# Linear attention and a squared-ReLU MLP on one core: batch 2's first matmul in the plain form, the last output matmul in another order, and new numbers in the planner

## The chip, the cores and the metric

The kernel runs on one core of a Trainium2 chip. Five engines work side by side, each on its own instructions in order: TensorE (PE in the profile; PEld is its loading of weights), VectorE (DVE), ScalarE (ACT), GpSimd (POOL) and SyncE (SP). DMA transfers are issued from the queues of SP, POOL and ACT. The metric is the device time of the core in microseconds (us), the median of several runs.

## The reference

There are 8 batches of 8 heads, 576 positions and 64 features per head. First comes a linear attention (no softmax), then a two-layer MLP over all 4608 rows of 512:

```python
def phi(x, c, s):                       # c, s: cos and sin of pi/2 * position / 576
    r = np.maximum(x, 0.0)
    return np.concatenate([r * c, r * s], axis=-1)
q_p, k_p = phi(q, cos_w, sin_w), phi(k, cos_w, sin_w)
kv  = einsum('bhsf,bhsd->bhfd', k_p, v);  z = k_p.sum(axis=2)
num = einsum('bhsf,bhfd->bhsd', q_p, kv)
den = einsum('bhsf,bhf->bhs', q_p, z)[..., None] + 1e-06
x   = (num / den)                       # heads side by side: 4608 x 512
h   = x @ w_in                          # 512 -> 2048
g   = np.maximum(h, 0.0) ** 2
out = g @ w_out                         # 2048 -> 512
```

## The kernel before

**Tiling.** Each batch has 512 main rows (four tiles j of 128) and 64 tail rows. The tails of all eight batches make a ninth block of 512 rows, m = 8, which goes through the MLP last. So the MLP has nine blocks of 512 rows; weights and activations are bf16, sums are float32 in PSUM (six banks numbered 0 to 5, and a pair called abank for the attention).

**The attention of a batch** (`plan_att`, L1005): SP loads v, k and q in halves (`load_half`, L176); ACT or DVE, whichever is free, make the cosine and sine features (`feat`, L278 and L282) and cast v (L300); TensorE forms kv and z in abank (`att_kv`, L324), ACT copies them out (L335); the features of q are transposed by a DMA on SP's queue (`att_qT`, L348), or by TensorE for some early tiles; `att_num` (L375) multiplies, `att_div` (L393 to L399) divides on DVE, and the result x is transposed again, by a DMA (`att_x`, L416) or by TensorE and a copy (L421, L425). Batch 1's x goes by TensorE.

**The MLP of a block** has a first matmul (`gemm1`) and an output matmul (`gemm2`). In the plain form, the first matmul is 16 units of 128 columns of w_in, each with 4 matmuls over all 512 rows (`unit_mm`, L460), an ACT relu (L469) and a DVE square of four units at a time (L477). In the other form the product of 2 x 2 blocks is made of seven block products instead of eight, numbered 1, 2, 5, 6, 7, 3, 4 in `plan_gemm1_7` (L864). It needs sums of blocks of w_in made once (`w1_sum`, L495; one of them overwrites a block of w_in), and of x for each batch (`x_sum`, L519). Per group of two column blocks there are seven products of 4 matmuls of 256 columns (`in_product`, L537), an ACT copy of product 5 (L907), two "seeds" in which ACT copies a partial sum from one bank to another (L896), two relus (L553), two DVE additions (L560), a maximum (L569) and one square (L477). There are four groups a batch. The output matmul has the same seven products (`product`, L686), each as two halves of 8 matmuls, with sums of the blocks of g (`g_sum`, L665) and of w_out (`w2_sum`, L646), a copy of product 5 (L977), two seeds (L951) and four result blocks (L957 on DVE, L961 on ACT). Blocks 0 and 1 have their first matmul in the plain form; `FIRST_7 = 2` (L1103) says that batch 2 is the first in the other. Block 0's output matmul is plain too (`first_out`, L602).

**The order of the work** after the first 17 us is made when the kernel is built. `Plan.add` notes each operation with its engine, a planned duration, what it reads and writes, and for TensorE's a due time. `Plan.order` (L55) goes through planned time: on the engine that is free first, of the operations that are ready, it takes the one with the earliest due time; due times are also passed back from what needs a result. An operation's result is ready a planned lag after its end (`LAG`, L23, or one of its own for a DMA). The order that comes out is the order of instructions on every engine. On the chip, the engines wait for each other's real results. Planned stages ("windows") follow each other: in window b there are the output matmul of block b, the first matmul of block b + 1 and the attention of batch b + 2.

**The end.** The last block's output matmul uses banks 0, 1 and 4. Its four result blocks are stored apart, each in two DMAs for 64 partitions (`put_part`, L631): two blocks on POOL's queue, one on SP's, and the last block one DMA on SP's and one on ACT's.

Of the kernel before, what the change touches and what calls it, by code (L numbers as in the profile page):

```python
# [9 lines left out]
ALU = mybir.AluOpType  # L10
# [8 lines left out]
class Plan:  # L19

    LAG = {"PE": 0.24, "ACT": 0.1, "DVE": 0.1, "POOL": 0.1, "SP": 0.1}  # L23

# [85 lines left out]
def kernel(  # L110
# [9 lines left out]
    nc = tc.nc  # L120
# [438 lines left out]
    def in_add(m, i, j, u, to):  # L559
# [65 lines left out]
    def put_part(i, eng, g, c0, c1):  # L625
        dst = bass.AP(
            tensor=out.tensor,
            offset=((4 * i + g) * S + MAIN) * DM + c0,
            ap=[[DM, TAIL], [2 * S * DM, 2], [1, c1 - c0]],
        )  # L630
        eng.dma_start(out=dst, in_=y_of(B, i)[g * TAIL : (g + 1) * TAIL, :, c0:c1])  # L631

    def w2_block(j, c):
# [92 lines left out]
    def plan_load(b, nm, after=0.0):  # L726
        for half in range(2):
            add("SP", 1.66, lambda half=half: load_half(nm, b, nc.sync, half),
                w=[(nm, half)], lag=2.0 + (CARE if b == 2 else CARE_IN), after=after)

    def plan_load_tail(b, nm, after=0.0):
        add("SP", 0.6, lambda: load_tail(nm, b, nc.sync), w=[(nm + "t", b % 2)], lag=2.0 + (CARE if b in (2, 3) and nm != "q" else CARE_IN), after=after)

# [59 lines left out]
    def plan_qT_pe(b, j, to, due, eng):  # L793
        slot = n_P[0] % 3
        n_P[0] += 1
        add("PE", 8 * 0.057, lambda: att_qT_pe(b, j, 0, H, to), r=q_parts((j,)), w=[("bank", to)], due=due)
        add(eng, cost(eng, 1024, "psum") if eng == "ACT" else 0.69, lambda: att_qT_copy(b, j, 0, H, to, ENG[eng]),
            r=[("bank", to)], w=[("qpTp", slot)])
        where[b, j] = ("qpTp", slot)
# [9 lines left out]
    def plan_x(b, i):  # L809
        js = (2 * i, 2 * i + 1) if i < J // 2 else (J,)  # L810
        w = [("xT", b % 2, j) for j in js] if i < J // 2 else [("xT8", b // 2)]
        if i < J // 2:
            add("SP", 1.5, lambda: att_x(b, i), r=[x_key(j) for j in js], w=w, lag=2.5 + CARE)
        else:
            add("SP", 1.2, lambda: att_x(b, i), r=[x_key(j) for j in js], w=w, lag=2.0 + CARE)

    def plan_x_pe(b, j, to, due, eng):
        add("PE", 4 * 0.057, lambda: att_x_pe(b, j, to), r=[x_key(j)], w=[("bank", to)], due=due)
        add(eng, cost(eng, 512, "psum") if eng == "ACT" else 0.42, lambda: att_x_copy(b, j, to, ENG[eng]),
            r=[("bank", to)], w=[("xT", b % 2, j)])  # L820
# [18 lines left out]
    def plan_gemm1(m, t, dt, banks, plain=False):  # L839
        order = list(range(HB)) if plain else [hb for h in range(HB2) for hb in (h, h + HB2)]  # L840
        for n, hb in enumerate(order):
            plan_unit(m, hb, banks[n % len(banks)], t + n * dt, halves=plain and n < 3)
            u = n // 4
            k = 2 if plain and u == 3 else 4
            if n % k == k - 1:
                a = n % 4 + 1 - k
                add("DVE", 0.15 + 512 * k * 0.00053, lambda u=u, a=a, k=k: square(m, u, plain, a, k),
                    w=[key for x in order[n + 1 - k : n + 1] for i in range(2) for key in g_keys(m, i, x // HB2, (x % HB2,))])
            if n % 4 == 3:
                if u >= 2 if plain else u % 2:  # L850
                    c = u - 2 if plain else u // 2
                    plan_g_sums(m, 4 * c, 4 * c + 4)

    def plan_w1_sums(after):
        first, second = [("w1", 0), ("w1", 1)], [("w1", 2), ("w1", 3)]
        for n, r, w in (
# [4 lines left out]
        ):  # L861
            add("DVE", 1.24, lambda n=n: w1_sum(n), r=r, w=w, after=after)

    def plan_gemm1_7(m, t, dt):  # L864
# [6 lines left out]
        for n, r, w in (  # L871
# [4 lines left out]
        ):  # L876
            add("DVE", 0.42, lambda n=n: x_sum(m, n), r=r, w=w)
        lo, hi = [("w1", 0), ("w1", 1)], [("w1", 2), ("w1", 3)]
# [5 lines left out]
        for u in range(HB2 // 2):  # L884
# [17 lines left out]
            def plus(a, i, j):  # L902
                add("DVE", 0.69, lambda u=u: in_add(m, i, j, u, a), r=[("bank", a)] + five, w=g(i, j))

# [5 lines left out]
            prod(6, Y)  # L910
            relu(X, 0, 0)
            seed(Y, X)
            prod(7, X)
            prod(3, Y)
            plus(X, 1, 1)
            plus(Y, 1, 0)
            prod(4, X)
            relu(X, 0, 1)
            add("DVE", 0.42, lambda u=u: in_max(m, u), w=g(1, 0) + g(1, 1))
            add("DVE", 1.24, lambda u=u: square(m, u, False), w=[key for i in range(2) for j in range(2) for key in g(i, j)])  # L920
            if u % 2:
                plan_g_sums(m, 2 * u - 2, 2 * u + 2)

    def plan_g_sums(m, h0, h1):
        hs = range(h0, h1)
        g = lambda i, j: g_keys(m, i, j, hs)
        s = lambda n: [("gs", n, h) for h in hs]
        dur = 0.15 + 256 * (h1 - h0) * 0.00053
        for n, r, w in (
# [7 lines left out]
    def plan_gemm2(m, t, dt):  # L937
# [35 lines left out]
        X, Y = (4, 5) if m < B else (0, 1)  # L973
        Z = X if m < B else 4
        prod(1, X)
        prod(5, Y)
        add("ACT", cost("ACT", 512, "psum"), lambda: nc.scalar.copy(out=five_of(m)[:, :, :], in_=half_bank(Y)),  # L977
            r=[("bank", Y)], w=[("five",)])
        seed(X, Y)
        prod(6, Y)  # L980
        prod(2, X)
        last(X, 0, 0, False)
        seed(Y, Z)
        if m == B:
            store_half(0, 0, ("POOL", "POOL"))
        prod(7, Z)
        prod(3, Y)
        last(Z, 1, 1, True)
        last(Y, 0, 1, True)
        if m < B:  # L990
            store(0)
        else:
            store_half(1, 1, ("POOL", "POOL"))
            store_half(0, 1, ("SP", "SP"))
        prod(4, Z)
        last(Z, 1, 0, False)
        if m == B:
            store_half(1, 0, ("SP", "ACT"))
        else:
            store(1)  # L1000

# [30 lines left out]

    for i, at in enumerate((16.0, 19.5, 22.0, 24.5)):
        plan.given["w1", i] = at
# [4 lines left out]
    tB = tA + HB * dtB  # L1039
    for nm, at in (("q", 30.0), ("k", 35.2), ("v", 40.0)):  # L1040
        plan.given.update({(nm, half): at for half in range(2)})
    plan.given.update({("kt", 1): 36.0, ("vt", 1): 40.5})
    for i, at in enumerate((33.0, 38.0, 42.5, 45.0)):
        plan.given["w2", i] = at

    def plan_first(s):
        half, hq = s // 4, s % 4
        js = (2 * half, 2 * half + 1)
        for a in range(2):
            to = 2 * (s % 2) + a  # L1050
            add("PE", 8 * 0.1092, lambda a=a: first_mm(s, P if s in (0, 4) else W, a),
                r=[("xT", 0, j) for j in js] + [("w1", hq)], w=[("bank", to)], due=T0 + (s + a / 2) * dt0)
            add("ACT", 0.59, lambda a=a: first_relu(s, a), r=[("bank", to)],
                w=[("g", 0, half, hb // HB2, hb % HB2) for hb in range(4 * hq + 2 * a, 4 * hq + 2 * a + 2)])
        add("DVE", 0.69, lambda: first_square(s),
            w=[("g", 0, half, hb // HB2, hb % HB2) for hb in range(4 * hq, 4 * hq + 4)])
# [33 lines left out]
    for n in range(1, 5):  # L1090
        for c in range(2):
            p = {1: 5, 2: 6, 3: 7, 4: 4}[n]
            before = {1: [], 2: [("w2t", 5, c)], 3: [], 4: [("w2t", 6, c)]}[n]
            add("DVE", 0.69, lambda n=n, c=c: w2_sum(n, 4 * c, 4 * c + 4),
                r=before + ([("w2", 2 + c)] if n == 3 else [("w2", c), ("w2", 2 + c)]),
# [15 lines left out]
    for b in range(2, B):  # L1111
# [108 lines left out]
```

## Time and profile before

| what | value |
|---|---|
| time, median of 3 runs | 284.98 us (284.95 to 285.75) |
| the profiled execution | 282.78 us, of which the span of instructions 281.0 us |
| TensorE busy | 267.0 us, 95% of the span |
| VectorE busy | 225.6 us, 80% |
| ScalarE busy | 196.8 us, 70% |
| granted clock of TensorE | 1.0 |
| moved by DMA | 53.38 MB, mean 190 GB/s |

The profile is one execution. Busy times are sums over instructions; matmuls overlap in the array, so the end shown for a matmul lies after the start of the next. In the lines of the timeline the columns are: start in us from the span's start, length, engine, line of the kernel, operation, what it writes and reads, the shapes, how many instructions the line merges, and in brackets the idle time of the engine before it with what ended it.

### The profile page before, as it was taken

The page shows a single profiled execution, that of the slowest core. Times are in us where ns is not written, and L with a number is a line of the kernel's source. Part 1 is how long each engine was busy: PE and PEld are TensorE (multiplying, and loading weights), DVE is VectorE, ACT ScalarE, POOL GpSimd, SP SyncE. Part 2 cuts the span into 40 slices and gives each one's busy share as a digit, 9 for nine tenths or more (in the row PEclk, how much of TensorE's full clock was granted, in tenths as well). Part 3 has the DMA queues.
Part 4 walks back from the last instruction along what each step waited for, and adds up shares of the span by engine and source line. Part 5 has one row for each costly group of instructions (what it writes and reads, how often), then busy time and mean ns, then how long its engine had stood idle before and what let it go on. Part 6 is the DMA issues. An engine that isn't in the chain of part 4 may idle for free.

```text
span 281.0 us, 6788 instructions
## 1 busy us (share of the span) xinstructions
PE 267.0 (95%) x2755; PEld 220.2 (78%) x2755; DVE 225.6 (80%) x437; ACT 196.8 (70%) x352; POOL 17.8 (6%) x31
## 2 busy tenths in 40 slices
PE   8899999799999979999999999999999999999793
PEld 3578955464779869888898899898988888888682
DVE  0966855989999998899989989997899779876701
ACT  2875862887997779999989999996526455555220
POOL 8345000000000000000000000000000000000011
PEclk9999999999999999999999999999999999999999
DMA  6999999999999999999899999474123001100305
GB/s 215 324 201 284 323 246 377 219 248 281 228 307 261 266 235 271 225 348 193 251 217 245 241 250 237 99 226 77 37 40 155 17 0 77 76 2 0 152 20 130
DMA packets 83534, 53.38 MB, mean 190 GB/s; under 512 B 55856, under 2 KB 79920, under 8 KB 83504
## 3 DMA queue, kind: packets, MB, share of 16 engines
q1 hardware_dynamic: 77376, 42.35, 60.8%
q0 software_dynamic: 5984, 10.49, 15.5%
q8 instruction: 21, 0.34, 0.5%
q10 hardware_dynamic: 144, 0.13, 0.1%
q14 instruction: 9, 0.07, 0.1%
HBM read 36.70 MB, written 9.44 MB: 164 GB/s over the span
## 4 chain that ended last, share of the span: by engine, by line
PE 72%; DMA 12%; ACT 7%; POOL 3%; issue 2%; SPq 1%; DVE 1%; POOLq 0%; ACTq 0%; DVEq 0%
PE bank L686 33%; PE bank L537 29%; DMA v<-in_v_dram 6%; PE bank L460 4%; DMA k<-in_k_dram 3%; PE abank L375 3%; DMA q<-in_q_dram 3%; PE abank L324 2%; SPq L176 1%; ACT kp L278 1%; ACT vext L300 1%; ACT qp L278 1%; ACT qpTp L907 1%; ACT bank L896 1%; PE bank L444 1%
## 5 line engine op out<-in xcount | busy, mean ns | idle before, releaser
L553 ACT ACTIVATE gT<-bank 128x512 bf16<-128x512 f32 x56 | 32.9, 599 | 33.4 <-PE bank L537 33.1
L686 PEld LDWEIGHTS <-gT 128*128 128x128 bf16 x512 | 49.3, 98 | 6.9 <-DVE gT L477 0.8
L537 PE MATMUL bank<-xT,w1sb 128*128 128x256 bf16 x336 | 48.9, 272 | 2.4 <-ACT bank L896 2.3
L686 PE MATMUL bank<-w2sb,gT 128*128 128x256 bf16 x384 | 49.8, 273 | 0.5 <-DVE gT L477 0.5
L537 PEld LDWEIGHTS <-w1sb 128*128 128x128 bf16 x448 | 42.7, 98 | 8.7 <-issue 3.4
L560 DVE TENSOR_TENSOR gT<-bank,qpTp 128x512 bf16<-128x512 f32 x56 | 37.6, 685 | 9.9 <-PE bank L537 8.5
L686 PEld LDWEIGHTS <-gs 128*128 128x128 bf16 x384 | 37.0, 98 | 6.5 <-issue 1.4
L477 DVE TENSOR_TENSOR gT<-gT 128x2048 bf16<-128x2048 bf16 (+1 forms) x33 | 38.9, 1187 | 3.9 <-ACT gT L553 3.5
L537 PEld LDWEIGHTS <-w1t 128*128 128x128 bf16 x336 | 32.4, 98 | 3.6
L686 PE MATMUL bank<-w2t,gs 128*128 128x256 bf16 x256 | 33.5, 273 | 1.3 <-ACT bank L951 1.3
L896 ACT COPY bank<-bank 128x512 f32<-128x512 f32 x56 | 32.4, 587 | 0.9 <-PE bank L537 0.5
L537 PE MATMUL bank<-qpTp,w1t 128*128 128x256 bf16 x224 | 32.8, 272 | 0.0
L399 DVE TENSOR_TENSOR x<-abank,rden 128x512 bf16<-128x512 f32 x31 | 21.4, 691 | 1.1
L957 DVE TENSOR_TENSOR ysb<-bank,y 128x512 f32<-128x512 f32 x16 | 11.0, 684 | 10.1 <-PE bank L686 9.9
L907 ACT COPY qpTp<-bank 128x512 f32<-128x512 f32 x28 | 16.3, 593 | 2.6 <-PE bank L537 2.4
L631 POOL DMA_DIRECT2D out_dram<-ysb x4 | 2.4, 614 | 245.3 <-ACT ysb L961 243.8
L278 ACT ACTIVATE kp<-k,sin_col 128x512 bf16<-128x512 f32 x23 | 16.3, 724 | 2.2 <-DMA k<-in_k_dram 2.2
L537 PE MATMUL bank<-xT,w1t 128*128 128x256 bf16 x112 | 16.8, 273 | 0.0
L537 PE MATMUL bank<-zeros,w1sb 128*128 128x256 bf16 x112 | 16.8, 272 | 0.0
L278 ACT ACTIVATE qp<-q,cos_col 128x512 bf16<-128x512 f32 x19 | 13.6, 722 | 4.4 <-DMA q<-in_q_dram 4.4
L686 PE MATMUL bank<-w2sb,gs 128*128 128x256 bf16 x128 | 16.6, 273 | 0.0
L686 PE MATMUL bank<-w2t,gT 128*128 128x256 bf16 x128 | 16.5, 273 | 0.0
(98 smaller groups left out, 414.9 us busy)
## 6 DMA issues: line engine op xcount, KB each, us to landing
out_dram<-ysb SPq DMA_DIRECT2D x16, 512.0 KB, 3.1
v<-in_v_dram SPq DMA_DIRECT2D x12, 512.0 KB, 6.3
q<-in_q_dram SPq DMA_DIRECT2D x12, 512.0 KB, 5.6
k<-in_k_dram SPq DMA_DIRECT2D x12, 512.0 KB, 6.1
v<-in_v_dram POOLq DMA_DIRECT2D x2, 1024.0 KB, 12.4
w1sb<-in_moe_w_in_dram POOLq DMA_DIRECT2D x4, 512.0 KB, 12.9
w2sb<-in_moe_w_out_dram POOLq DMA_DIRECT2D x4, 512.0 KB, 15.4
k<-in_k_dram SPq DMA_DIRECT2D x1, 1024.0 KB, 6.1
```

The lines of the kernel that those rows point to most:

```text
L278: eng.activation(out=dst[ps, :, lo : lo + D], in_=src[ps], func=ACTF.Relu, scale=col[ps])
L375: nc.tensor.matmul(out=num[half][ps, hh * E1 : (hh + 1) * E1], lhsT=qpT[half][:, hh, ps], rhs=kvzs[b2][:, half * HH + hh, :], start=True, ...
L399: nc.vector.tensor_tensor(out=x[:, a:z], in0=n4[:, :, :, 0:D].rearrange("p b (k l) d -> p b k l d", l=2), in1=rden[:, a:z] .rearrange("p b ...
L460: nc.tensor.matmul(out=out_, lhsT=w1sb[:, kb, hb * P : (hb + 1) * P], rhs=x_block(m, kb), start=(kb == 0), stop=(kb == KB - 1),)
L477: nc.vector.tensor_tensor(out=g, in0=g, in1=g, op=ALU.mult)
L537: nc.tensor.matmul(out=bank[to][:, s * W : (s + 1) * W], lhsT=lhs[:, kb, (2 * u + s) * P : (2 * u + s + 1) * P], rhs=rhs[:, kb, :], start= ...
L553: nc.scalar.activation(out=g_pair(m, i, j, u), in_=bank[to][:, :].rearrange("p (s c) -> p s c", s=2), func=ACTF.Relu,)
L560: nc.vector.tensor_tensor(out=g_pair(m, i, j, u), in0=bank[to][:, :].rearrange("p (s c) -> p s c", s=2), in1=in_five(u).rearrange("p (s c) ...
L686: nc.tensor.matmul(out=bank[to][:, s * DM2 : (s + 1) * DM2], lhsT=lhs[:, hb, s * P : (s + 1) * P], rhs=rhs[:, hb, :], start=(fresh and hb ...
L896: add("ACT", psum, lambda: nc.scalar.copy(out=bank[b][:, :], in_=bank[a][:, :]), r=[("bank", a)], w=[("bank", b)])
L907: add("ACT", psum, lambda u=u, Y=Y: nc.scalar.copy(out=in_five(u), in_=bank[Y][:, :]), r=[("bank", Y)], w=five)
L957: lambda: nc.vector.tensor_tensor(out=y_view(m, i, cc), in0=half_bank(a), in1=five_of(m)[:, :, :], op=ALU.add),
```

## The change

Three things change. `FIRST_7` goes from 2 to 3, so batch 2's first matmul takes the plain form and the sums of w_in are made for batch 3. In block 8, the last group of the first matmul squares its blocks apart, and the output matmul adds its products in the order 1, 2, 6, 5, 7, 3, 4 with banks 0, 1, 5 and 4; its last result block is copied in two halves and stored in four DMAs, three on SP's queue and one on ACT's. The planner's durations, lags, arrival times of loads, and some due times get other numbers; the due times of batch 1's attention become earlier. A branch for `FIRST_7 == 1` is added that isn't taken.

```diff
-    LAG = {"PE": 0.24, "ACT": 0.1, "DVE": 0.1, "POOL": 0.1, "SP": 0.1}
+    LAG = {"PE": 0.31, "ACT": 0.15, "DVE": 0.14, "POOL": 0.1, "SP": 0.1}
...
+    def square_block(m, i, j, u):
+        g = g_pair(m, i, j, u)
+        nc.vector.tensor_tensor(out=g, in0=g, in1=g, op=ALU.mult)
+
+    def square_half(m, u):
+        g = gT_of(m).rearrange("p (j h) c -> p j h c", j=2)[:, :, 2 * u : 2 * u + 2, W : 2 * W]
+        nc.vector.tensor_tensor(out=g, in0=g, in1=g, op=ALU.mult)
...
+    def put_quarter(i, eng, g, s_, c0, c1):
+        dst = bass.AP(
+            tensor=out.tensor,
+            offset=((4 * i + 2 * s_ + g) * S + MAIN) * DM + c0,
+            ap=[[DM, TAIL], [1, c1 - c0]],
+        )
+        eng.dma_start(out=dst, in_=y_of(B, i)[g * TAIL : (g + 1) * TAIL, s_, c0:c1])
+
+    def last_copy(s_, to):
+        nc.scalar.copy(out=y_view(B, 1, 0)[:, s_, :], in_=half_bank(to)[:, s_, :])
...
         if kind == "feat":
-            return {"ACT": 0.2 + 0.00083 * n, "DVE": 0.16 + 0.0005 * n}[eng]
+            return {"ACT": 0.185 + 0.00083 * n, "DVE": 0.14 + 0.0005 * n}[eng]
         if kind == "cast":
-            return {"ACT": 0.19 + 0.00083 * n, "DVE": 0.09 + 0.00077 * n}[eng]
+            return {"ACT": 0.095 + 0.00083 * n, "DVE": 0.08 + 0.0005 * n}[eng]
         if kind == "psum":
-            return {"ACT": 0.155 + 0.00085 * n, "DVE": 0.15 + 0.00105 * n}[eng]
-        return 0.15 + 0.00053 * n
+            return {"ACT": 0.045 + 0.00085 * n, "DVE": 0.06 + 0.00105 * n}[eng]
+        return 0.06 + 0.00053 * n
...
-        add("SP", 2.95 if i < J // 2 else 1.48, lambda: att_qT(b, i), r=q_parts(js),
-            w=[("qpT", i)], lag=CARE + (1.3 if i < J // 2 else 2.5))
+        add("SP", 2.0 if i < J // 2 else 1.5, lambda: att_qT(b, i), r=q_parts(js),
+            w=[("qpT", i)], lag=CARE + (2.4 if i < J // 2 else 1.7))
...
             prod(4, X)
+            if apart:
+                add("DVE", 0.34, lambda u=u: in_max(m, u), w=g(1, 0) + g(1, 1))
+                add("DVE", 0.60, lambda u=u: square_half(m, u), w=g(1, 0) + g(1, 1))
             relu(X, 0, 1)
+            block(0, 1)
...
+        X, Y, Z, V = 0, 1, 5, 4
         prod(1, X)
         seed(X, Y)
         prod(2, X)
         last(X, 0, 0, False)
+        store_half(0, 0, ("POOL", "POOL"))
+        prod(6, Y)
         seed(Y, Z)
+        prod(5, V)
+        five(V)
         prod(7, Z)
+        last(Z, 1, 1, True)
+        store_half(1, 1, ("POOL", "POOL"))
         prod(3, Y)
         last(Y, 0, 1, True)
+        store_half(0, 1, ("SP", "SP"))
         prod(4, Z)
+        for sub in range(2):
+            add("ACT", cost("ACT", 256, "psum"), lambda sub=sub: last_copy(sub, Z),
+                r=[("bank", Z)], w=[("y", 1, 0, sub)])
+            for g, q in enumerate(("SP", "ACT") if sub else ("SP", "SP")):
+                add(q, 0.6, lambda g=g, q=q, sub=sub: put_quarter(1, ENG[q], g, sub, 0, DM2),
+                    r=[("y", 1, 0, sub)], w=[("out", m, 1, 0, g, sub)])
...
-        plan_num(1, j, tA + (10.5 + 1.5 * j) * dtB)
+        plan_num(1, j, tA + (6.0 + 1.0 * j) * dtB)
         if j == 0:
-            plan_qT_pe(1, 3, 2, tA + 12 * dtB, "DVE")
-        plan_x_pe(1, j, 3, tA + (11.5 + 1.5 * j) * dtB, "ACT" if j % 2 else "DVE")
+            plan_qT_pe(1, 3, 2, tA + 7 * dtB, "DVE")
+        plan_x_pe(1, j, 3, tA + (7.2 + 1.0 * j) * dtB, "ACT" if j % 2 else "DVE")
...
-    win[0] = (t, t + HB * dC)
-    plan_gemm1(1, t, dC, (2, 0, 1, 3), True)
-    t += HB * dC
-    FIRST_7, STRIDE, SHIFT = 2, 2.0, -6.0
+    win[0] = (t, t + 14.0)
+    FIRST_7, STRIDE, SHIFT = 3, 2.0, -6.0
...
+        plan_gemm1(1, t, dC, (2, 0, 1, 3), True)
+        t += HB * dC
...
         if m == FIRST_7:
-            plan_w1_sums(win[m - 2][0])
+            plan_w1_sums(28.0 if m == 2 else win[m - 2][0])
```

More of the change, by code (lines that the diff above doesn't have):

```diff
@@ L861, in plan_w1_sums @@
         ):
-            add("DVE", 1.24, lambda n=n: w1_sum(n), r=r, w=w, after=after)
+            add("DVE", 1.14, lambda n=n: w1_sum(n), r=r, w=w, after=after)
     def plan_gemm1_7(m, t, dt):
@@ L902, in plus, with block @@
             def plus(a, i, j):
-                add("DVE", 0.69, lambda u=u: in_add(m, i, j, u, a), r=[("bank", a)] + five, w=g(i, j))
+                add("DVE", 0.60, lambda u=u: in_add(m, i, j, u, a), r=[("bank", a)] + five, w=g(i, j))
+            apart = m == B and u == HB2 // 2 - 1
+            def block(i, j):
+                if apart:
+                    add("DVE", 0.34, lambda u=u: square_block(m, i, j, u), w=g(i, j))
             prod(1, X)
@@ L911, in plan_gemm1_7 @@
             relu(X, 0, 0)
+            block(0, 0)
             seed(Y, X)
@@ L917, in plan_gemm1_7 @@
             prod(4, X)
+            if apart:
+                add("DVE", 0.34, lambda u=u: in_max(m, u), w=g(1, 0) + g(1, 1))
+                add("DVE", 0.60, lambda u=u: square_half(m, u), w=g(1, 0) + g(1, 1))
             relu(X, 0, 1)
-            add("DVE", 0.42, lambda u=u: in_max(m, u), w=g(1, 0) + g(1, 1))
-            add("DVE", 1.24, lambda u=u: square(m, u, False), w=[key for i in range(2) for j in range(2) for key in g(i, j)])
+            block(0, 1)
+            if not apart:
+                add("DVE", 0.34, lambda u=u: in_max(m, u), w=g(1, 0) + g(1, 1))
+            if not apart:
+                add("DVE", 1.14, lambda u=u: square(m, u, False), w=[key for i in range(2) for j in range(2) for key in g(i, j)])
             if u % 2:
```

80 lines of the change are left out of this document (44 added, 36 removed).

## The prediction

> **What bounds the kernel now.** I read the page's busy shares first, then a table of busy time by stretches, then the waits of TensorE alone, and last the timeline around each of those waits.
>
> ```profile
> span 281.0 us, 6788 instructions
> PE 267.0 (95%) x2755; PEld 220.2 (78%) x2755; DVE 225.6 (80%) x437; ACT 196.8 (70%) x352; POOL 17.8 (6%) x31
> ```
>
> TensorE is busy for 95% of the span, so this is a TensorE-bound kernel; what can be won is the few places where it stands idle, and what can be lost is any matmul added. The stretches say where those places are (columns: stretch, length, busy time and count of PE, PEld, DVE, ACT, POOL, then clock, DMA share, GB/s):
>
> ```profile
> 52.00:58.00 6.00, 4.06 (x66) 3.07 (x64) 5.85 (x12) 5.14 (x10) 0.00 (x0) 1.00 1.20 186
> 72.00:100.00 28.00, 27.33 (x315) 23.43 (x314) 26.74 (x54) 24.24 (x45) 0.00 (x0) 1.00 1.09 260
> 100.00:106.00 6.00, 4.34 (x41) 3.74 (x40) 5.95 (x11) 5.01 (x10) 0.00 (x0) 1.00 0.98 234
> 106.00:178.00 72.00, 71.91 (x818) 64.08 (x816) 65.88 (x133) 67.86 (x124) 0.00 (x0) 1.00 1.05 246
> 178.00:256.00 78.00, 77.97 (x773) 69.35 (x771) 67.03 (x115) 47.44 (x87) 0.00 (x0) 1.00 0.25 67
> ```
>
> From 106 to 256 us TensorE idles for 0.12 us in 150: there a better order can give nothing, and a worse one can only cost. The idle time lies at 52-58 (1.94 us), 72-100 (0.67), 100-106 (1.66) and in the tail after 256. The waits of TensorE and the timeline name each:
>
> ```profile
> PE bank L537 <- ACT bank L896: 2.3, 3, 1.7
> PE bank L686 <- ACT bank L951: 1.3, 1, 1.3
> PE bank L686 <- DVE gT L477: 0.5, 1, 0.5
> ```
>
> ```profile
> 53.62 0.72 ACT L278 ACTIVATE kp<-k,cos_col 128x512 bf16<-128x512 f32 x1 [0.54 <-DMA k<-in_k_dram]
> ...
> 54.70 0.38 PE L421 MATMUL bank<-ident,x 128*128 128x128 bf16 x4 [0.96 <-DVE xT L425]
> ...
> 56.24 1.03 PE L324 MATMUL abank<-vext,kp 128*128 128x65 bf16 x24 [0.81 <-ACT kp L278]
> ```
>
> ```profile
> 104.79 0.60 PE L537 MATMUL bank<-xT,w1sb 128*128 128x256 bf16 x4 [1.66 <-ACT bank L896]
> ```
>
> ```profile
> 262.98 0.39 PE L686 MATMUL bank<-w2sb,gT 128*128 128x256 bf16 x2 [0.53 <-DVE gT L477]
> ...
> 267.34 1.03 PE L686 MATMUL bank<-w2t,gs 128*128 128x256 bf16 x8 [1.27 <-ACT bank L951]
> ...
> 275.24 2.36 SPq L631 DMA_DIRECT2D out_dram<-ysb  x3
> 276.39 0.59 ACT L961 COPY ysb<-bank 128x512 f32<-128x512 f32 x1 [4.78 <-PE bank L686]
> 277.01 0.74 ACTq L631 DMA_DIRECT2D out_dram<-ysb  x1
> ```
>
> In brackets stands the idle time before the row and what ended it. One matmul of 256 columns starts 0.109 us after the one before it (12 of them take 1.31 us in the chain), but its end is shown 0.27 us after its start; so a wait costs the idle time shown plus 0.16. The two at 54.70 and 56.24 cost about 2.1 us, those at 78.41 and 81.13 (0.35 and 0.32 shown) 1.0, the one at 104.79 1.8, the two of the tail 2.1.
>
> **Part 1: batch 2's first matmul, seven products to plain.** Removed: 4 groups of 7 products of 4 matmuls, 112 x 0.109 = 12.2 us. Added: 16 units of 4 matmuls of 512 columns, each 0.216 (12 of them in 2.59 us in the chain), 64 x 0.216 = 13.8 us. Cost: **+1.6 us** of TensorE, on the path, because TensorE is what is full there; no wait hides it. ACT loses 20 operations (4 copies, 8 seeds, 8 relus) and gains 16 relus, all about 0.49 from start to start: -1.9 us. DVE loses 8 additions of 0.60, 4 maxima and 4 block sums of 0.334: -7.5 us, and gets 4.5 us (4 sums of w1 at 1.14) that ran at 51.9, 57.1, 60.7 and 72.0 and now lie one stage later. All of that is beside TensorE, in a stretch where DVE is busy 26.7 of 28 us; so the waits at 78 and 81, where ACT's seeds came late, go with the seeds. But the sum of w1 that overwrites its own source must still wait for the last plain unit, on DVE's queue, with the block sums of the next batch behind it: at 71.98 that was the start of the trouble at 75-81, and it moves to the end of the next stage, about 100. There the wait at 104.79 stood already. I take it that the two bad passages (1.0 and 1.8) become one of 0.9, between none and 2.8: **-1.9 us**.
>
> **Part 2: the planner's numbers.** The new costs are the distance from start to start in the trace: ACT's copy of 512 out of PSUM 0.48 (was planned 0.59), DVE's 0.60 (0.69), the square of 2048 1.135 (1.24). The only moved steps whose effect I can place are batch 1's: its attention products, due 44.1 + 1.8j, are now due 38.7 + 1.2j. In the trace they run at 43.99, 47.05, 50.11 and 52.74, spread between output matmuls that were not waiting for anything; the chain of one (0.41 on TensorE, then 1.3 of DVE) allows one each 1.8, so the last comes near 49, and batch 1's units have their input when the output matmuls end near 51. The sum of w1 at 51.89 also leaves DVE's queue, and the copy at 54.23 that TensorE waited for at 54.70 no longer stands behind it. That wait goes (1.1). The second waits for batch 2's k, which landed at 53.52 and needs eight feature passes; the load's place is unchanged, so this wait is late next, in part behind units that can now run: 0.2 of its 1.0. Together **-1.3**, ends 0 and -2.1. Everything else that the new numbers reorder (SP's transposes, planned at 2.0 instead of 2.95, its loads, ACT's and DVE's choice of feature passes) I can't follow; in 106-256 there is 0.12 us to win, so it can only cost: I take +0.3, with ends 0 and +4.2 (below).
>
> **Part 3: the tail.** The last first-matmul group squares its blocks one by one: 0.334 + 0.334 + 0.60 against 1.135, +0.13 on DVE, but the first output product needs only the block whose relu ended at 257.2, so the wait at 262.98 goes. The output product order becomes 1, 2, 6, 5, 7, 3, 4 over four banks, and the fifth product has a bank of its own, with nothing waiting in line for its copy and for the seed (0.59 + 0.57, the wait at 267.34): whichever of 2, 6 and 5 is ready can cover each seed, and I cost both seeds at 0. If no product is ready beside a seed, that cover is gone and one seed costs 0.8. Same 14 half products of 0.87: TensorE ends 2.1 us earlier, at 274.25 by this profile. What is late next is SP. Before, its queue issued two stores at 275.24, and one at 277.00 when the last copy was done. Now it has five: two for the block of product 3, whose sum is done near 273.25, two for the first half of the last block, one for the second half. At 0.62 to 0.68 from issue to issue they begin at 273.3, 274.0, 274.65, 275.3 and 276.0. The last one starts 1.0 earlier than before, not 2.1, whatever the split copy gains (two copies of 256, each between 0.2 and 0.59, done near 275, before SP can use them). POOL's four issues stay. A store of 128 KB landed 2.3 to 3.4 after its issue; for 64 KB I take 0.3 less than the last one's 2.5, between 0 and 0.6. Tail: **-1.3 us**, ends 0 and -2.1.
>
> The Trainium skill, DMA: Bandwidth & Descriptors, Issuing engines are not separate DMA queues, says that issuing on several engines saves sequencer time only, "usually small relative to the DMA itself". By that rule SP's five issues would not matter and the tail would give the full 2.1, 281.6 in all. In this trace three issues take 2.36 us of queue against a landing of 2.5, which is not small, so the sum keeps the rows.
>
> **The sum.** +1.6 - 1.9 - 1.3 + 0.3 - 1.3 = -2.6. The profiled execution took 282.78 us (span 281.0 and 1.78 around it), so it would become 280.2. The median of the three runs, 284.98, stands 2.2 above that execution; I keep that distance: **282.4 us**.
>
> **Rivals.**
> Slower: a plan without padding. The old costs were some 0.1 us too long for each ACT and DVE operation, which left slack between what TensorE is ordered to do and when its input is there. Without it, each later passage to a new batch (about 130, 157, 184, 210 and 237) could get a wait like that at 104.79. Half of it each, 0.83 x 5 = 4.2 in place of my 0.3, gives 286.3. It decides from 0.75 us a passage on ((285.83 - 282.4 + 0.3) / 5). For it: ACT and DVE are 94% and 92% busy at 106-178, so a late one has little room to catch up. Against: the new costs agree with the distances in the trace, and the lags got longer, TensorE's 0.24 to 0.31.
> No change: batch 2's x is late. A plain unit reads both transposed halves, which landed at 69.16 and 73.39; the seven products could begin at 70.91 with the first. If the second lands no earlier, what was won at 52-58 is lost again (0 for -1.3), two products (0.87) that filled 70.9-73.4 are missing, and the passage near 100 keeps its 1.8 (only -1.0 won): 1.6 - 1.0 + 0.9 + 0.3 - 1.3 = +0.5, 285.5. Against it: batch 2's attention runs behind the same earlier steps, so its x should come earlier too.
> More is won: all four early waits go whole (2.1 + 1.0 + 1.8), no new ones, and SP's queue doesn't count (-1.9): 1.6 - 4.9 - 1.9 = -5.2, 279.8.
>
> **How the numbers follow.** A change under 0.3% (0.85 us) can't be told from none here. The forecast as summed has 0.51 (its own range 281.0 to 284.3, mostly under 284.13); the slower rival 0.20; no change 0.17; more won 0.12. Faster by over 0.3% takes 0.12, 0.49 of the forecast and 0.02 of the third: 0.63. Slower takes 0.19 and 0.04: 0.23. Same 0.14. The range goes from the best case to the slower rival's half-wait price: 279.8 to 286.3.
>
> **What would show it.** Part 1: batch 2 has 64 matmuls of 512 columns more than before, no seed (L896's operation) between 72 and 98, and TensorE without idle rows there. Part 2: the transposes of batch 1's x end by about 50, and TensorE's idle time at 52-58 falls from 1.94 to about 1. Part 3: no idle row of TensorE between 258 and its end, and SP's five last stores back to back, the last issue about 1.7 us after TensorE's end instead of 0.6. It is wrong if TensorE shows idle time at 106-256, if the first plain units of batch 2 wait for a transpose of x, or if the sum of w1 in its own place makes TensorE wait over 1 us near 100.

## The result and the profile after

The changed kernel takes 281.72 us (median of 4 runs, 281.40 to 282.92) against 284.97 us before, run beside it: a ratio of 0.9893, 95% interval 0.9855 to 0.9932. (Every ratio compares a kernel's runs with those of the kernel before in the same series; runs more than 1.5% above the fastest of their kernel are left out.) The forecast was 282.4, range 279.8 to 286.3.

The two profiled executions hide that: their spans are 281.0 and 281.1 us. The one of before was 2.2 us shorter than its median and the one of after 1.2 us longer. About 1.1 us of this lies in the first 12 us, which the change doesn't touch: TensorE's first attention products began at 10.66 us in the profile of before, and between 11.00 and 11.80 us in every later profile, whatever the kernel; they wait for batch 0's v, which landed (had arrived whole) at 10.08 there and at 11.23 in the profile of after. So the two profiles are compared place by place, not by their ends.

Busy shares of the changed kernel:

```profile
span 281.1 us, 6673 instructions
PE 267.1 (95%) x2702; PEld 214.5 (76%) x2707; DVE 224.4 (80%) x442; ACT 185.5 (66%) x330; POOL 18.2 (6%) x31
```

The same stretches of the changed kernel as those shown of before:

```profile
52.00:58.00 6.00, 5.95 (x67) 4.10 (x66) 5.47 (x13) 6.00 (x13) 0.00 (x0) 1.00 0.84 204
...
72.00:100.00 28.00, 25.39 (x233) 16.29 (x231) 26.05 (x52) 21.70 (x38) 0.00 (x0) 1.00 1.11 252
100.00:106.00 6.00, 5.25 (x65) 3.82 (x63) 3.02 (x8) 4.32 (x9) 0.00 (x0) 1.00 1.02 209
106.00:178.00 72.00, 70.98 (x786) 62.39 (x785) 66.68 (x131) 60.00 (x110) 0.00 (x0) 1.00 0.99 248
178.00:256.00 78.00, 78.00 (x780) 69.56 (x779) 65.84 (x117) 45.17 (x84) 0.00 (x0) 1.00 0.26 71
```

TensorE's idle time at 52-58 fell from 1.94 us to 0.05, and at 100-106 from 1.66 to 0.75. But at 72-100 it rose from 0.67 to 2.61, and at 106-178 from 0.09 to 1.02. What it waits for is now something else. TensorE's waits in the changed kernel (in total, times, longest):

```profile
PE abank L324 <- DVE vext L300: 2.2, 1, 2.2
PE bank L537 <- DMA xT<-x: 1.4, 2, 0.9
PE bank L460 <- DMA xT<-x: 1.3, 1, 1.3
PE bank L306 <- DVE zeros L201: 1.2, 1, 1.2
PE bank L537 <- DVE qpTp L519: 0.8, 1, 0.8
PE bank L705 <- DVE gs L684: 0.7, 1, 0.7
```

Before, ACT's seeds (L896, L951) led this list with 3.6 us; not one is left. In their place stand transfers of x (`xT<-x`), and the block sums of x that need them (L519). The first and fourth lines are the start of the kernel.

The timeline of the changed kernel where batch 2's first units begin:

```profile
70.11 2.51 SPq L416 DMA_TRANSPOSE xT<-x  x1
...
73.30 1.48 PE L705 MATMUL bank<-w2t,gs 128*128 128x256 bf16 x12 [0.71 <-DVE gs L684]
...
76.09 2.76 PE L460 MATMUL bank<-xT,w1sb 128*128 128x512 bf16 x12 [1.31 <-DMA xT<-x]
```

TensorE got to these units early and stood still until the second half of batch 2's x, issued at 70.11, had landed at 76.05. And the tail of the changed kernel:

```profile
274.58 1.91 PE L705 MATMUL bank<-w2t,gT 128*128 128x256 bf16 x16
...
275.37 1.34 SPq L639 DMA_DIRECT2D out_dram<-ysb  x2
276.52 0.65 ACT L650 COPY ysb<-bank 128x256 f32<-128x256 f32 x2 [4.78 <-PE bank L705]
276.92 1.78 SPq L647 DMA_DIRECT2D out_dram<-ysb  x3
277.20 0.56 ACTq L647 DMA_DIRECT2D out_dram<-ysb  x1
```

No row of TensorE after 256 shows idle time any more. The last 112 matmuls of the output product take 12.52 us, against 14.73 before. From TensorE's end to the end of the span it is 4.65 us, against 4.64.

### The profile page after: what moved, and what is told of

Read it like the earlier page. It is cut to its first block, busy times and chain, and to the rows that moved or that the text cites. A ratio compares the mean times of both kernels' runs of the same rounds, so it can differ in the third digit from the quotient of the medians.

```text
span 281.1 us, 6673 instructions
## 1 busy us (share of the span) xinstructions
PE 267.1 (95%) x2702; PEld 214.5 (76%) x2707; DVE 224.4 (80%) x442; ACT 185.5 (66%) x330; POOL 18.2 (6%) x31
## 4 chain that ended last, share of the span: by engine, by line
PE 79%; DMA 10%; DVE 5%; issue 1%; POOL 1%; SPq 1%; ACT 1%; POOLq 0%; DVEq 0%
PE bank L705 30%; PE bank L537 24%; PE bank L460 6%; PE bank L610 5%; PE bank L585 5%; DMA xT<-x 5%; PE abank L324 3%; DMA q<-in_q_dram 3%; PE abank L375 3%; DMA v<-in_v_dram 2%; PE bank L357 1%; DVE gT L477 1%; SPq L176 1%; PE bank L444 1%; PE bank L421 1%
## 5 line engine op out<-in xcount | busy, mean ns | idle before, releaser
L553 ACT ACTIVATE gT<-bank 128x512 bf16<-128x512 f32 x48 | 28.4, 600 | 31.4 <-PE bank L537 30.8
L537 PE MATMUL bank<-xT,w1sb 128*128 128x256 bf16 x288 | 42.4, 273 | 1.4 <-DMA xT<-x 1.4
L537 PEld LDWEIGHTS <-w1sb 128*128 128x128 bf16 x384 | 36.8, 98 | 6.6 <-DMA xT<-x 2.0
L560 DVE TENSOR_TENSOR gT<-bank,qpTp 128x512 bf16<-128x512 f32 x48 | 32.1, 685 | 6.9 <-PE bank L537 5.0
L537 PEld LDWEIGHTS <-w1t 128*128 128x128 bf16 x288 | 27.1, 98 | 4.5 <-DVE qpTp L519 1.2
L537 PE MATMUL bank<-qpTp,w1t 128*128 128x256 bf16 x192 | 28.3, 273 | 0.8 <-DVE qpTp L519 0.8
L460 PE MATMUL bank<-xT,w1sb 128*128 128x512 bf16 x116 | 27.8, 379 | 1.3 <-DMA xT<-x 1.3
L916 ACT COPY bank<-bank 128x512 f32<-128x512 f32 x48 | 27.8, 588 | 0.5
L469 ACT ACTIVATE gT<-bank 128x512 bf16<-128x512 f32 x32 | 18.9, 596 | 9.8 <-PE bank L460 9.5
L460 PEld LDWEIGHTS <-w1sb 128*128 128x128 bf16 x116 | 10.5, 98 | 11.5 <-DMA xT<-x 1.6
L933 ACT COPY qpTp<-bank 128x512 f32<-128x512 f32 x24 | 14.2, 598 | 5.2 <-PE bank L537 5.0
L994 ACT COPY ysb<-bank 128x512 f32<-128x512 f32 x15 | 8.8, 588 | 11.2 <-PE bank L705 10.9
```

Source lines behind the costliest of these rows:

```text
L460: nc.tensor.matmul(out=out_, lhsT=w1sb[:, kb, hb * P : (hb + 1) * P], rhs=x_block(m, kb), start=(kb == 0), stop=(kb == KB - 1),)
L469: nc.scalar.activation(out=gT_of(m)[:, hb, :], in_=bank[to][:, :], func=ACTF.Relu)
L537: nc.tensor.matmul(out=bank[to][:, s * W : (s + 1) * W], lhsT=lhs[:, kb, (2 * u + s) * P : (2 * u + s + 1) * P], rhs=rhs[:, kb, :], start= ...
L553: nc.scalar.activation(out=g_pair(m, i, j, u), in_=bank[to][:, :].rearrange("p (s c) -> p s c", s=2), func=ACTF.Relu,)
L560: nc.vector.tensor_tensor(out=g_pair(m, i, j, u), in0=bank[to][:, :].rearrange("p (s c) -> p s c", s=2), in1=in_five(u).rearrange("p (s c) ...
L916: add("ACT", psum, lambda: nc.scalar.copy(out=bank[b][:, :], in_=bank[a][:, :]), r=[("bank", a)], w=[("bank", b)])
```

## The experiments

**The three parts, alone and in pairs.** Part 1 is batch 2's plain first matmul, part 2 the planner's numbers, part 3 the tail. Six kernels make all combinations.

Part 3 alone, with the old planner numbers:

```diff
 (before)
+    square_block, square_half, put_quarter, last_copy and their use for m == B
+        X, Y, Z, V = 0, 1, 5, 4        # products 1, 2, 6, 5, 7, 3, 4
```

> The kernel before, with part 3 alone (squares of the last group apart, the last output matmul in its new order and banks, four last stores), planned with the old numbers. If the tail gives what the two profiles show (the last output matmul takes 12.52 us of TensorE's time instead of 14.73, and the last landing keeps its distance to TensorE's end), the time falls by 2.2, to a ratio of 0.992. If SP's queue takes back what I priced (1.0 later issue, 0.3 shorter landing), it falls by 1.3, ratio 0.995. If the tail owes its gain to the new planner numbers too, TensorE still waits there: under 0.8, ratio 0.997 or more.

Measured: 0.9908 (0.9863 to 0.9953). TensorE's waits in its profile:

```profile
...
PE bank L537 <- ACT bank L915: 2.3, 3, 1.7
PE bank L306 <- DVE zeros L201: 1.2, 1, 1.2
PE bank L421 <- DVE xT L425: 0.9, 1, 0.9
```

The waits of the middle stand as before (the seeds of the first matmul, here at L915, with the same 2.3 us), those of the tail are gone, and the last 112 matmuls take 12.52 us. The first of the three expectations holds in the trace: TensorE's 2.2 us are won whole, and without the new numbers. The time agrees (0.9922 would be 2.2 us), but its interval also holds the 0.995 of the second expectation.

Part 1 alone:

```diff
 (before)
-    FIRST_7, STRIDE, SHIFT = 2, 2.0, -6.0
+    FIRST_7, STRIDE, SHIFT = 3, 2.0, -6.0
```

> The kernel before, with part 1 alone (batch 2's first matmul plain, old numbers, old tail). Theory: 1.6 us of matmuls are added, the waits at 78, 81 and 105 go in part, and the plain units wait for the second transposed half of x; net -0.5 to +1.5, ratio 0.998 to 1.005. Rival, that relief of ACT and DVE is the win of the whole change: -2 us or better, ratio 0.993 or less, and TensorE without idle rows at 72-106.

Measured: 0.9979 (0.9946 to 1.0012), a gain of about 0.6 us that the interval doesn't separate from none. Its profile shows what pays for the 1.6 us of added matmuls: TensorE's idle time from 60 to 108 falls from 2.33 to 0.42 us, and no row of TensorE waits for batch 2's x. My theory had the plain units wait for the second half of x, which they don't do here. The rival, that relieving ACT and DVE is the win of the whole, falls by the time.

Part 2 alone:

```diff
 (before)
-    LAG = {"PE": 0.24, "ACT": 0.1, "DVE": 0.1, "POOL": 0.1, "SP": 0.1}
+    LAG = {"PE": 0.31, "ACT": 0.15, "DVE": 0.14, "POOL": 0.1, "SP": 0.1}
 ... and all planned costs, arrival times, batch 1's due times, win[0] as in the change
```

> The kernel before, with part 2 alone (the planner's numbers, windows and due times; FIRST_7 stays 2, old tail). Theory: TensorE's idle time at 52-58 goes from 1.94 to under 0.3, and waits of TensorE for transposes of x appear behind it that give a part back; net -0.5 to -2, ratio 0.993 to 0.998. Rival (a plan without padding costs more than the passage gives): ratio 1.001 or more, with idle TensorE at 106-256 of over 2 us.

Measured: 1.0062 (1.0023 to 1.0102), 1.8 us slower. TensorE's waits in its profile:

```profile
PE bank L537 <- DVE qpTp L519: 1.7, 2, 1.3
PE bank L537 <- DMA xT<-x: 1.6, 1, 1.6
PE abank L375 <- DMA qpT<-qp: 1.4, 1, 1.4
PE bank L686 <- ACT bank L952: 1.3, 1, 1.3
```

The time of the rival came out, with its mechanism only in part: at 108-256 the profile shows 1.8 us idle, under the 2 that I had named. The larger part is transfers: 1.6 us at 71.72 for the first half of batch 2's x, 1.4 at 92.48 for a transpose of q.

The pairs:

```diff
 tail_first7:    before + part 1 + part 3
 numbers_first7: before + part 1 + part 2
 numbers_tail:   before + part 2 + part 3
```

> Parts 1 and 3 without part 2: the kernel before with batch 2's first matmul plain and the new tail, planned with the old numbers. Alone, part 3 gave a ratio of 0.991 and part 1 0.998. If the parts add, this gives 0.989, as much as the whole change, and the new numbers are worth nothing; if the new numbers are needed to make the plain form pay (the rival), it stays at 0.991 or more and the whole change is ahead of it.

Measured: 0.9887 (0.9835 to 0.9938). The parts add, and without the new numbers the kernel is as fast as with them, as far as intervals of half a per cent can tell.

> Parts 1 and 2 without part 3: the changed kernel with the old tail. The whole change gave 0.990, the tail alone 0.991. Theory: the tail is worth its 2.2 us here too, so this stands near 0.998 (0.995 to 1.001), although the numbers alone gave 1.006: the plain form takes the seeds and block sums out of the stretch where the new plan makes TensorE wait. Rival, that the parts simply add (1.006 x 0.998): 1.004.

Measured: 0.9948 (0.9916 to 0.9981), at the lower end of the theory's range. The time shows no harm from the new numbers once batch 2 has the plain form.

> Parts 2 and 3 without part 1: the changed kernel with batch 2's first matmul in the seven products again. It is the last of the eight combinations. Alone, the numbers gave a ratio of 1.006 and the tail 0.991; with the plain form the numbers did no such harm (1 and 2 together 0.995, 1 and 3 0.989, all three 0.990). If the parts add: 0.997 (0.993 to 1.001), and the plain form is worth 0.7% under the new numbers, against 0.2% under the old ones. Rival: the numbers' harm came from the old tail or from one odd series, and this stands at 0.991 or less.

Measured: 0.9963 (0.9927 to 0.9998), as the sum has it. So the harm of the numbers under the seven products is no accident of one series. Its profile has the same wait in the same place:

```profile
71.03 0.60 PE L537 MATMUL bank<-xT,w1sb 128*128 128x256 bf16 x4 [1.65 <-DMA xT<-x]
```

All eight, with TensorE's idle time in one profile each, summed over the rows of the trace (us):

| kernel | ratio | 52-60 | 60-108 | 108-256 | after 256 |
|---|---|---|---|---|---|
| before | 1 | 1.94 | 2.33 | 0.11 | 1.81 |
| part 3 (tail) | 0.9908 | 2.03 | 2.33 | 1.35 | 0 |
| part 1 (plain form) | 0.9979 | 1.41 | 0.42 | 1.33 | 1.81 |
| part 2 (numbers) | 1.0062 | 0.72 | 4.08 | 1.82 | 1.29 |
| 1 and 3 | 0.9887 | 1.51 | 0.41 | 2.87 | 0 |
| 1 and 2 | 0.9948 | 0.05 | 3.69 | 0.49 | 1.29 |
| 2 and 3 | 0.9963 | 0.62 | 4.68 | 2.55 | 0 |
| all | 0.9893 | 0.05 | 3.36 | 1.02 | 0 |

The column 52-60 is the gain of the numbers, the column 60-108 what takes it back. The kernel with the tail alone runs the order of before up to the tail, so its row is a second profile of that order: 1.35 us idle at 108-256, where the first profile had 0.11. So a difference of that size in the column 108-256 says nothing about a part.

Idle time alone doesn't give the balance of the numbers beside the plain form, where 60-108 gets 2.9 to 3.3 us worse and the time doesn't. Counted from the first MLP matmul, TensorE reaches batch 1's output products after 52.2 us with the new numbers and after 53.9 and 54.9 with the old ones. It has done with batch 4's after 168.8 and 169.1 with the new, 167.6 and 170.5 with the old. The lead of 1.7 to 2.7 us is gone there.

**The changed kernel again.**

```diff
 (after, unchanged)
```

> The changed kernel, unchanged, once more beside the other three. In its first profile TensorE began the first attention products at 11.74 us, in the profile of before at 10.66, though both kernels have the same instructions up to there; its other runs were 1.2 to 1.5 us shorter than the profiled one. Theory: this start varies with the landing of batch 0's v and is no part of the change, so another profile can have it at 10.7. Rival: it is later in every run of the changed kernel. The ratio should again be 0.986 to 0.993, and the waits for transposes of x at 76, 99, 103 and 129 should stand again if they are the kernel's own (3.5 us shown in all), or move if they come from one execution's transfers.

Measured: 0.9896 (0.9860 to 0.9931). The start was at 11.36, so the 10.7 of the theory did not come again. Nor is it the change that makes the start late: with the tail alone it was at 11.80, with part 1 alone at 11.62. TensorE's wait for the second half of x stands, and is longer:

```profile
PE bank L460 <- DMA xT<-x: 2.4, 1, 2.4
```

The waits at 99 and 129 nearly go (0.2 us for the two together, after 0.60 and 0.85; 0.39 and 0.36 in the kernel of parts 1 and 2): their size changes with the execution. The one at 74-76 is the kernel's own, and so is the one at 103, where TensorE waits for block sums of batch 3's x (0.75 us in both profiles).

**Batch 2's products due earlier.**

```diff
-            plan_num(b, j, t + (0.36 + 0.09 * j) * w)
+            plan_num(b, j, t + (0.36 + 0.09 * j) * w - (5.0 if b == 2 else 0.0))
```

> The changed kernel with one edit: the attention products of batch 2 are due 5 us earlier in the plan. In both profiles of the changed kernel TensorE waits at 74 to 76 us for the second transposed half of batch 2's x (1.31 and 2.36 us shown), whose DMA was issued at 70.1 and 70.4, right after the last of those products, which ran between units of the first matmul at 60.6, 63.5, 66.3 and 68.3. Theory: the products were late because the plan gave them late due times; now they run by 66, the half lands near 72, the wait goes, and the time falls by 1 to 2.5 us against the changed kernel: ratio to before 0.981 to 0.987. Rival: the transposes are slow because the DMA queues are full, and land late anyway, or the next batch takes the wait over (at 99 to 103): ratio 0.988 or more.

Measured: 0.9884 (0.9831 to 0.9936); the wait is still there, 1.90 us at 76.25, and the two transposes were issued at 65.3 and 69.7, as in the changed kernel (66.1 and 70.1 there with a later start, 65.2 and 70.4 in its second profile). Theory wrong: late due times are not what holds the products back. Only the first of the four ran sooner, 41.7 us after the first MLP matmul for 42.6; the other three ran at 45.4, 48.3 and 50.2 as in the changed kernel. So this run doesn't show what earlier products would have done.

**The second half of batch 2's x without a DMA.**

```diff
+            if b == 2 and j >= 2:
+                plan_x_pe(b, j, 2 + j, t + (0.45 + 0.09 * j) * w, "DVE" if j == 2 else "ACT")
-            if j % 2:
+            elif j % 2:
                 plan_x(b, j // 2)
```

> The changed kernel, but the second half of batch 2's x (tiles 2 and 3) is transposed by TensorE and copied by DVE and ACT, in the banks 4 and 5, and not by a DMA. Cost: 8 transposes and two copies, about 0.5 us of TensorE. Theory: in the changed kernel the time won at 52-58 is lost again to the wait for this half (1.1 to 2.4 us shown at 74-76 in five profiles, and 0.7 for a sum of g just before it); without the DMA the wait goes and the time falls by 0.6 to 2.0 us, ratio to before 0.982 to 0.988. Rival, that the next wait takes its place (the sums of g at 72, batch 3's x at 99 to 103, which hangs on transfers that keep their pace): ratio 0.989 or more, with the waits at 99-103 longer by what was won.

Measured: 0.9882 (0.9843 to 0.9921), at the edge between the two. What the profile shows:

```profile
72.87 1.47 PE L460 MATMUL bank<-xT,w1sb 128*128 128x512 bf16 x6 [1.01 <-DMA xT<-x]
```

TensorE now waits for the first half instead, 1.01 us, which landed at 72.83. The idle time at 60-108 is 1.16 us instead of 3.36 and 3.98, and from the first MLP matmul to TensorE's end it takes 256.1 us, against 258.4 and 258.1 in the two profiles of the changed kernel (257.5 with batch 2's products due earlier). In the times the gain can't be told from none: 0.9882 against the changed kernel's 0.9893 and 0.9896.

The same edit with the old numbers:

```diff
 before + part 1 + part 3, and the lines above
```

> Parts 1 and 3 with the old planner numbers, and the second half of batch 2's x by TensorE as well. With the old numbers the profile shows no wait of TensorE for this half, since TensorE reaches it 2.8 us later (first output product of batch 1 at 72.67 against 70.25 and 69.70). Theory: the edit then wins nothing and costs its 0.5 us of TensorE, ratio 0.989 to 0.991. Rival: it also spares DMA time in a crowded stretch and wins 0.5 or more, ratio 0.987 or less.

Measured: 0.9899 (0.9851 to 0.9947), in the theory's range, but the interval reaches into the rival's as well. The one profile would speak for a gain: 256.9 us from the first MLP matmul to TensorE's end, against 260.0 with parts 1 and 3. So whether the edit wins anything under the old numbers stays open.

**Batch 3's k held back.**

```diff
-            plan_load(b, nm, hold)
+            plan_load(b, nm, 68.0 if (b, nm) == (3, "k") else hold)
```

> The changed kernel with one edit: the two loads of batch 3's k are held back in the plan until 68 (in the changed kernel they were issued at 62.0 and 62.6 and moved 1 MB just before the transposes of batch 2's x, whose first half then took 6.5 us from issue to landing and 7.4 to 7.9 in four later profiles, against 6.0 in the kernel before; later batches' halves took 3.0 to 4.6). Theory: the transposes are slow because they queue behind these loads; without them the first half takes about 5, the second lands by 74, and TensorE's wait at 74-76 shrinks to under 0.7; total -0.5 to -1.5 if k's later landing stops nobody, ratio 0.984 to 0.989. Rival: the transposes take as long without the loads, wait and time stay (ratio 0.989 to 0.991), or the features of k come late and the time grows.

Measured: 1.0022 (0.9986 to 1.0058), about 3.6 us worse than the changed kernel. TensorE's waits for x grew, and that for the block sums of x to 1.4 us:

```profile
PE bank L460 <- DMA xT<-x: 2.9, 1, 2.9
PE bank L537 <- DMA xT<-x: 1.8, 1, 1.8
...
```

The transpose took 8.1 us from issue to landing. But the edit hadn't made room: with k gone, the planner put batch 0's two stores of 512 KB there. What the trace says of SP's queue ahead of the first transpose of batch 2's x, in four kernels:

| kernel | issued | ahead of it on SP's queue | the last of these landed | it landed |
|---|---|---|---|---|
| before | 63.19 | q, v, v | 68.14 | 69.16 |
| parts 1 and 3 | 66.67 | q, v, v | 69.90 | 70.82 |
| all | 66.14 | q, k, k, v | 71.64 | 72.61 |
| all, k held | 65.52 | q, v, two stores | 72.61 | 73.61 |

It lands 0.9 to 1.0 us after the transfer ahead of it, whatever its own issue time. The second half does the same: in the changed kernel the stores ahead of it landed at 75.05, it at 76.05. So neither theory is settled as I had put it: with the two stores in k's place as many bytes stood ahead as before, and x landed no sooner.

What the new numbers do here can be read from the order of SP's issues, first in the kernel before, then in the changed one:

```profile
63.19 2.26 SPq L416 DMA_TRANSPOSE xT<-x  x1
...
65.54 1.19 SPq L176 DMA_DIRECT2D k<-in_k_dram  x2
```

```profile
62.02 1.58 SPq L176 DMA_DIRECT2D k<-in_k_dram  x2
...
66.14 2.53 SPq L416 DMA_TRANSPOSE xT<-x  x1
```

With the old numbers batch 3's k is issued behind the first transpose of x, with the new ones ahead of it. It is so in all eight combinations. In them the first half lands 52.0 to 53.1 us after the first MLP matmul with the old numbers, and 53.8 to 55.2 with the new ones (55.6 in the second profile of the changed kernel). So x comes later while TensorE comes sooner. That the amount of data ahead makes it late is read from the traces; a kernel with that place left empty was not tried. Nor do the runs tell a limit of the queue from a lack of free DMA engines: at 58-74 all but 0.02 MB of the changed kernel's traffic is on SP's queue, and the mean share of the 16 DMA engines is given as 1.07, so they were busy nearly all the time. (The expectation leaves out that batch 3's first half took 5.6 us too, in the changed kernel.)

**The last block copied whole.**

```diff
-        for sub in range(2):
-            add("ACT", cost("ACT", 256, "psum"), lambda sub=sub: last_copy(sub, Z),
-            ...
+        last(Z, 1, 0, False)
+        store_half(1, 0, ("SP", "ACT"))
```

> The changed kernel with the last result block copied whole and stored by two DMAs of 128 KB (one on SP's queue, one on ACT's), as before. In the profile of the changed kernel both half copies waited for the last matmul (276.52 and 276.79 for an end of TensorE at 276.49), so the split starts nothing earlier, and it puts two more issues on SP's queue, the last one 1.66 us after TensorE's end instead of 0.65. Theory A (SP's queue costs): the whole copy is 0 to 0.6 us faster. Theory B (a small store lands sooner: 2.0 us for 64 KB against 2.85): the two are equal within 0.3 us, since the distance from TensorE's end to the span's end was 4.65 in both kernels.

Measured: 0.9884 (0.9820 to 0.9949), against 0.9893 and 0.9896. Its tail:

```profile
273.27 1.91 PE L705 MATMUL bank<-w2t,gT 128*128 128x256 bf16 x16
...
274.06 2.36 SPq L639 DMA_DIRECT2D out_dram<-ysb  x3
275.21 0.59 ACT L994 COPY ysb<-bank 128x512 f32<-128x512 f32 x1 [4.78 <-PE bank L705]
275.83 0.74 ACTq L639 DMA_DIRECT2D out_dram<-ysb  x1
```

From TensorE's end to the last landing it is 3.53 us here (275.17 to 278.70), 3.68 with the split (276.49 to 280.17), 3.50 before. To the end of the span it is 4.68, 4.65 and 4.64: after the last landing SP still takes 0.97 to 1.15 us, and the kernel that lands later takes the shorter one. Theory B: the two are equal, the split copy and its four stores cost 0.15 us at most up to the landing, nothing at the span's end, and win nothing. The split's idea, to copy one half while the other is being made, doesn't happen: both copies start after the last matmul, though the eight matmuls of the first half had ended at 275.61. The Trainium skill, PSUM — Partial Sum Buffer, PSUM bank collisions raise a hardware error, says to guard PSUM by bank and quadrant of partitions, more simply by bank, and not by address. The kernel's waits agree with that: the first copy waits for the semaphore of the last of the 16 matmuls, and the two start at 276.52 and 276.79 for an end of TensorE at 276.49. What an unguarded read would do no run here shows.

## Why the prediction was right or wrong

The sum was right, 282.4 for 281.7, and two of its three terms were not. Part 2 brought about 1 us less than forecast and part 3 about 0.9 us more, so that the sum came out is luck. Of the three signs by which I had said it would be wrong, two came: idle time of TensorE at 106-256 (1.02 us; but the second profile of before's order has 1.35), and the first plain units of batch 2 waiting for a transpose of x.

**Part 1, -0.3 (+1.6 - 1.9): right, as far as the runs can tell.** Alone it gave -0.2%, about -0.6 us, with an interval that also holds none. The added matmuls are there, batch 2's seeds are gone, and with the old numbers the idle time at 60-108 fell by 1.9 us shown. Counted as the prediction counts a wait, shown time plus 0.16, that is 2.3 for the 1.9 forecast: not even the one bad passage that I had left in came. The in-place sum of w1, feared near 100, ran at 105.19 in the changed kernel without TensorE waiting for it.

**Part 2, -1.3 + 0.3: wrong.** The step "that wait goes" held, and more: the second wait at 56 went too, and the idle time at 52-58 fell by the full 1.9. The step that failed is the 0.3 for everything else that the new numbers reorder, SP's loads and transposes among it. TensorE got to batch 1's output products 3.2 us sooner after its first MLP matmul (70.25 less 18.05, against 72.21 less 16.86; 0.4 of it is a product of batch 2 that ran ahead of them before), and then waited for x, 1.1 to 2.4 us, and 0.7 for sums of g. That is the mechanism of my "no change" rival, which I had given 0.17: what is won at 52-58 is lost again at the transposes. What I had held against it, that batch 2's x should come earlier too, is the reason that failed: x came later, behind batch 3's k on SP's queue. The numbers alone cost 0.6%; beside the plain form they give -0.3% under the old tail and nothing under the new one, both within the intervals. The rival of a plan without padding has the ratio that I gave it for the numbers alone (1.006, for 1.001 or more), but its place, the later passages, was not the larger part of it.

**Part 3, -1.3: the mechanism right, a term mis-sized.** The two waits went (2.2 us for 2.1), SP's five stores came nearly back to back (it waited 0.2 us for the first half's copy, which I had thought would be done in time), and the last issue came 1.67 us after TensorE's end, for 1.7 predicted. What I mis-sized is the landing behind it. I let the last issue, 1.0 us earlier than before where TensorE's end was 2.1 earlier, decide, with a landing 0.3 shorter than 2.5. But 2.5 was SP's last store; the one that had landed last before was ACT's, 2.85 us after its issue, and the last one now lands 2.01 us after its own. So up to the last landing the queue costs 0.2 us of the 2.2, and not 0.8, and at the end of the span nothing is left of it (4.65 us after TensorE's end, against 4.64). The Trainium skill's rule on issuing engines, which I set aside for the rows, gave the better number: its 2.1 for the tail is nearly what was measured, 2.2. The runs don't bear out its reason, since the last issue did come 1.0 us later after TensorE's end, and the shorter landing made up for it. (The landings of 128 KB stores in the trace before are 2.3 to 3.2 us, not up to 3.4; the sum doesn't use that.)

The profile that the prediction read was a good execution, 2.2 us under the median: its start was 0.3 to 1.1 us earlier than in all later profiles, and at 108-256 it had 0.11 us of idle time where the same order later had 1.35. So "there a better order can give nothing" was read from one good case.

So the gain that stands by itself is the tail's. The plain form's 0.2% can't be told from none under the old numbers; under the new ones it is 0.7% to 1.1%, because there it undoes their harm. Parts 1 and 3 together give 0.9887, the whole change 0.9893. Why the transposes hold batch 2 is shown as far as the queue: what stands ahead of them. Whether another order of SP's queue would give the early gain back stays open.

## What to carry to other kernels

An engine that is full and gets ahead in one place meets what was hidden there: before a wait is counted as won, look up how late the next input lands, in time after the engine gets there, and what stands ahead of it in its DMA queue. At the end of a kernel count back from the end through the last landing, not from the last issue: a smaller store that starts later can land in the same time. And when a change has several parts, one part can pay for another's loss; the time of the sum doesn't say which.

## What the runs showed of the hardware

- A DMA transpose of two tiles of x on SP's queue took 3.0 to 3.5 us from issue to landing after 200 us, where the DMA engines moved 58 GB/s, and 3.9 to 8.3 us when issued at 63 to 72, where they moved 230 to 330; there the first half landed 0.9 to 1.1 us after the transfer ahead of it, in all fourteen profiles.
- A store of 64 KB on SP's queue at the end landed 2.0 to 2.5 us after its issue, one of 128 KB 2.5 to 3.2 us. Behind the last landing the span went on for 0.97 us with the four small stores and 1.14 with the two large ones.
- The start of the kernel, up to TensorE's first attention product, took 10.66 us in one execution and 11.00 to 11.80 in thirteen others with the same instructions there: profiles of two kernels should be lined up at a common instruction before their ends are compared.
